# Block-sparse attention and a gated convolution FFN on one core: the same steps in a new written order

## The chip, the cores and the metric

The kernel runs on one core of a Trainium2 chip. Five engines of the core take part: TensorE (PE) multiplies matrices, VectorE (DVE) and ScalarE (ACT) compute element by element and move data between memories, GpSimd (POOL) starts loads, SyncE (SP) starts stores and transposing transfers. Each engine works through its own list of instructions in order; semaphores make one wait for another. The metric is device time in microseconds, median of three runs: 207.86 (207.11 to 208.13).

## The reference

Two operations, one after the other. The first is attention over 4 batches, 8 heads, 768 positions, head size 64, with a mask by blocks of 32 positions:

```python
scores = scale * np.matmul(q, k.transpose(0, 1, 3, 2))
mask = np.abs(blk_i - blk_j) <= 1          # neighbours, first and last block,
mask = mask | ...                          # and three sampled blocks per block row
attn = softmax(np.where(mask, scores, -1e9))
x = np.matmul(attn, v)                     # heads side by side: (4, 768, 512)
```

The second is a feed-forward network whose hidden layer is gated by a convolution over three positions:

```python
h = np.maximum(x @ w_in, 0.0)              # (4, 768, 1024)
conv_out = sum(conv_w[k] * hp[:, k:k + S, :] for k in range(3))
gate = 1.0 / (1.0 + np.exp(-conv_out))
out = h * gate @ w_out                     # (4, 768, 512)
```

## The kernel before

**Tiling.** Heads go in 16 pairs, four pairs to a batch. The output positions go in segments: each batch has two halves of 384 positions, and the last half of the last batch is cut in 256 and 128, nine segments in all. Within a segment, blocks of 128 keys by 128 queries are taken eight at a time; such a *unit* has one score tile `st` of 1024 columns. There are 144 units, 18 to a whole segment.

**A unit.** TensorE computes its scores from the slot `t` of the head pair, which holds transposed K and Q with 24 rows of mask appended (L762, two steps `s` of four blocks). ACT takes the exponential into `pt` (L774). TensorE multiplies by V (L799, two steps `av` of four matmuls with 65 columns, the 65th being the sum). When a head pair of a segment is done, DVE takes the reciprocal (L707) and normalises (L709) into `xtok`.

**Ahead of the units.** POOL's queue loads K, Q and V with a cast to bf16 (`nat`, `nq`, `vn`; L239). For the first six pairs TensorE transposes K and Q (L460, L500, L522) and DVE or ACT copies them into the slot (L331, L327). For the other ten, SP's queue transposes them by DMA into `stg` (L597), and DVE copies from there. V is copied to `vt` (L327 on ACT, L331 on DVE). Mask rows are computed on DVE at the start (L299 and others), written back once by SP to `mback` (L343), and filled into reused slots from there.

**The FFN.** `xtok` is transposed to `xT`, by TensorE for the first and the last two segments (L728, with a copy on ACT or DVE), by SP's DMA otherwise (L718). The first FFN matmul (L896) goes to a `mix` tile; ReLU copies it to `hE`, on ACT (L916) or DVE (L918). DVE makes three products with the convolution weights (L954) and two sums (L962), ACT a tanh (L1001), DVE the rest of the gate (L1004) and the gate product `gT` (L1009). For the last, 128-wide segment TensorE does the convolution itself with diagonal matrices (L379 makes them, L973 uses them). The second FFN matmul (L831) goes to `mix` again (to `st` for the last block); an output copy by ACT (L327) or DVE (L331) brings it to `o2s`, and SP stores it (L840).

**Buffers.** PSUM holds two `st`, two `av` and two `mix` tiles. `mix` is shared by transposes and both FFN matmuls.

**The order.** The code first builds a graph of 1,787 steps and then emits them by a written list: `ORDER` is a text in which two characters name a step, one may choose the engine, and one chooses the buffer. `put_down` reads it from left to right. What each engine does in which order is set by this text alone; nothing is planned at run time. At the start TensorE has 13 matmuls on zeros with 256 columns and 32 with 128 (L230); the text places these fillers too. POOL has `pace` copies between its loads (L407, L673): tiny copies that wait for an exponential or for an earlier load, so that loads start no earlier.

Of the kernel before, what the change touches and what calls it, by code (L numbers as in the profile page):

```python
# [22 lines left out]
1SA05j11V15k0E5g15c05d1Y05l211V18V191WV11XV5o05p5q35h1k15i0F1+V1ZV5t15u0G5m0H5n5C05D1O02k1/12d22x31b1a2v21l24V1  # L23
0I0J5r5v45s4S5E55H15I2702a15M05N5J05O10K5R15S5T25w5x15F5G28V22bV2cV29V5+05/5K5L5P6035y02iV21t5z1o631642l1654680
692o05Q6d16e5U2mV32nV2pV2qV6a55V5A16i06j6f06106266671c5W12y5BV06r16s6k11u1P06b6c4T2r34U2J04V2L04W1v2M6t26w05X6x
6y36g2016h6B16C6D46l1RV1QV2wV36m16G06H6u1s1n6v6z5Y06I51p4X1w4Y2X14Z1x4+2Z14/2+501y511z5234222V5ZV21V6n26P16Q6R0
6A6E6F6U06V6J6K1j6o6L06M6p06W16S06Z16+6T6N16qV6OV1r6/2720732e02fV2gV743ih16X77178iiik07f07g794il1q7k17l7h51i
ijV002KV47m0in16Y707p07q7r1imViF0iGiHiI71ioipV17u17v7w2iJiq0ir7C075762z1isViK2AV42BV7D7H17I7E32C07a7b17i7j7niN1
7c17J42s17M07N2tV7o7s7t7x537R17S2DV2uV2EViO147y7O57z2iP7AiQiz1iLiR7T03007W07X7Y17diAit082183iBA2842iu870887F17G
ivV37K7L2N18938c18d7PiM07Q7U7V2OV02PViw07e1iS312/18h0ixiyV8i7Z7+0852Q17/0iV2iW8e48j58p18q3823j38r0868a8b8f8u08v  # L30
2SViT80iYiX8w18g8k8l8z18A2RV7BiC08s18B28E08FiD8G3iU8J18K8L4iEVj918R08S8tja8x8T58y8C8D8W18H8X8I36254378/090iZi+
j13jf0jg8Y09112YV0j28m18nj4j333V32Vi/941958M8N08U8V8Z8+92939c09d962j5j01mj63919h19ijh979e498jbj7j89j5ji158O29m0
9n9r19sjc818ojjA09o1jdA13ajo0jp9w09t29909a35V18P3f3g33cV3bV553i3d0562F057jl1jmjnA9x9E19FjqV3eV2jJ08Q23k09y3ju0
jv9f09g9J0jKjM9K9G0jLjwVjN9k9l9p3h3o2T13p19q9L49O19Pjr19u2G09T09U9v9z2HV2IV9Q5jO9B19Cjs9/1jx09A19V2jyjzAa0a139D
9b3r3s0jtVjR1jSjP3w1jUjA1jBa402U0jCA3l9Ha5a91aaa619I9M9NjD1jEae09Raf9Sab42VV2WVaj1jFAjZ2jTjVjQj+ag53u3tjWak9W9X
jG0a20jH9Y2k09Zj/al0jIAar0a3a7a8kv13Dacasadaw1axjXjYkj0ahat3ay1aB0aiamaCan1auavkk3E13G3Ak1k53k6k7k8k9k29+k3k4
aD4kaaG1aHao1azaAkwaI5aO0aEaFaPklkx3B23F3M3N0aQ2aT1aUaV0kbkckmknV23nVapaJkyaY0aZb11b2aK3v43xkzA33qV33zV3yVa+3
b31kE0kFkB1kCb60b7aR0aS3H0aL0be1kDV14kGAkZ0k+k/l0kK0kLbfaWb84kMAbg5kH1kIbj0kJV53I1bkkQ0l1bl2kRkSAbo1kT13P3Q23S
kAjekobpaXbt0a/bub0b4l2bq03mVaMl51l6bv3kN0kOb5kUl8kPV6ld2bB1bCb9ba1bb2bD1kVA7kW0bG0bHbhkXbI4bibmbnbL1brl73R3XbM
bcbsbwbxbQ0bRaq03T0jkaNkYAbN5bS2kd1bd3JbE0bFkebV1bWkp0lelfl9lall3c10l3lg3CV4lhkqbJbKkrl41by1lbbObPbX0c2c61lic33  # L40
3UkfkgkhA3bzlmljlolnlplcc7c813OV0bAkslqlk3LVbTbUlz1bYcb0ccbZ1c4cg1lrls3KV3VV13WVcd4ktA1b+0b/c5c9cachci5lAlBcelC
lDA2co0cpct1cfculI0lF1lGlHVlJlKVm10cjm2m4cq0cv3cy0czm3m5cD1ckcEcA4cF53+3/343403Y141kilt1lL0cr0cl2cmcI0lMlNAcscJ
lulO0lPcwcQ1cK2cR4c4d0m6lQVm91mam7mbmcm8cS1lvlwcxcV0cWcBcCcG3ZV1c+1c/cHlxA0cX3d04lR0cL42494hd30d4c01441cN1mdcO
d50lSlU1cM1lTAlVdb1dccTcUmelWVmh2mimfdg0lX0dhl+1mklYl/dd5lZVdl1cYcZdi2d1dmd2d6d7de0m0Adn1cnmjmgku4i0dq0drd80mp3
d9mrmlmqmsmx0ds3lE4e4fdv1mtdwmD1dfdx4mmmElycP45dD0dEdI1djdkdF5dodpdtdJdudymydN0dadz1dGdHdOmnmudK24q4r1dP1dA2mo
mFmzdBmvmwdS1dT46V247VdU3mAmBV34a24gd+0d/mGdLe31dMdQe4mHV1e04e52dC24jmY0e80mV1e9mWdRed1dVeemZdW4v4n4s4tea04E4F2
mXV08m+VdX1nh0njdY4w1ei0n21n3ejm/0n0ef5e10eq1ere2e6e7ebdZmI4o0ek14Jn1A94bV2ev0n50ecewes4ninkn4Anlegehex2np1el
em1eA1eBeC0en0nq4kV3eonsepn6etn7Aaeun81n9eF0eGeN1eOnaAnx2eyezeDnb0nceH5eS0eEeTeInrnt4lVeP1eJne1eX1eYeQ0eK2eL4u
4m4xnyndAbeU4eZ2nmnunznfnAmJ0mKeRngVnF3nGnB4pV3f00eVeMmLf1f51eWf6nvnnnHno0f25mP1mQmMfd0fef71mNA2ff4nCnInwnJ4yV4
mRe+e/fi1mSfjf34zVnDmTA0fn0f4o30o4fk2o5Ao61foo7fs1ftfp54G4Bo8Vot0ounEov4C14H4I4PnKnL4Q2fu3nN0nOf8f91fa1nMnT1ow  # L50
fA0fBnUfgnPfF1nVmC4K0484LoxfbfC04DA4fGfH1oyfhnQnRV1fK0nWflfLnZ0fmnXV3n+fc04RV0oz4MV04NVo01o1fP1fM4fQfU0fqfrfvfV
fwn/Ao2AfR2oAol1omfx0onfW5oofyopfD0oc0g01g1g23o91fEodg50oeAg6g70oqfInSoafJobVoB2oDoCof0ga1fNgbfOgc1fSoggf0ggoi1
# [1005 lines left out]
```

## Time and profile before

| | |
|---|---|
| median of three runs | 207.86 us (207.11 to 208.13) |
| profiled execution, first to last instruction | 205.4 us; the page has no other time for it |
| median less span | 2.46 us |
| TensorE busy | 197.1 us |
| ACT busy | 189.7 us |
| DVE busy | 184.9 us |
| POOL busy | 59.4 us |
| moved by DMA | 25.6 MB |

In the profile a row of the timeline gives start, duration, engine, line, operation, output and input, and the count of instructions that it merges. A row of the windows gives the stretch, its length, then busy time and count for each engine, the granted TensorE clock, the DMA share and the rate. A row of the groups gives line, engine, shapes and count, then busy time and the mean of one in ns, then the idle time ahead and what ended it. The chain of waits lists pieces that follow one another, each freed by the one ahead. TensorE's matmuls overlap: each lasts longer than the distance to the next.

### The profile page before, as it was taken

What the parts mean: (1) busy time and instruction counts of PE and PEld (TensorE: products, weight loads), DVE (VectorE), ACT (ScalarE), POOL (GpSimd) and SP (SyncE); (2) the same over time, 40 slices, a digit from 0 to 9 for tenths busy, and PEclk for the clock granted to TensorE, in tenths of its full rate; (3) what the DMA queues carried; (4) which work ended last, traced back from release to release, by engine and by line L of the source; (5) the groups of instructions that cost most, each with busy time, mean ns of one, the idle gap of its engine ahead of it and who ended that gap; (6) DMA issues with size and microseconds to landing.
All of it is one profiled execution on the core that took longest, in us unless ns stands there. A gap on an engine that the chain in (4) does not pass through costs nothing.

```text
span 205.4 us, 6237 instructions
## 1 busy us (share of the span) xinstructions
PE 197.1 (96%) x2392; PEld 142.3 (69%) x2409; DVE 184.9 (90%) x572; ACT 189.7 (92%) x253; POOL 59.4 (29%) x113
## 2 busy tenths in 40 slices
PE   7799999999999999999999999999999999999992
PEld 5677877786667766776667767766567667787760
DVE  7999999999999998999899996999999959999960
ACT  6799999999999999999999998999999978998841
POOL 8689255312831133202443253900000000000000
PEclk9999999999999999999999999999999999999999
DMA  5999999994999979999779799998053131000405
GB/s 155 196 190 154 186 178 114 197 127 88 154 150 126 125 103 138 218 166 163 95 105 226 97 117 123 175 154 126 14 174 88 21 123 51 3 2 3 153 3 204
DMA packets 50969, 25.59 MB, mean 125 GB/s; under 512 B 36764, under 2 KB 47996, under 8 KB 50940
## 3 DMA queue, kind: packets, MB, share of 16 engines
q0 software_dynamic: 19728, 11.05, 46.0%
q1 hardware_dynamic: 30924, 13.86, 31.0%
q8 instruction: 19, 0.31, 0.6%
q10 hardware_dynamic: 288, 0.30, 0.5%
q14 instruction: 10, 0.08, 0.1%
HBM read 23.09 MB, written 6.29 MB: 143 GB/s over the span
## 4 chain that ended last, share of the span: by engine, by line
PE 68%; ACT 15%; DVE 12%; issue 3%; ACTq 0%; DVEq 0%
PE st L762 22%; PE mix L896 15%; PE mix L831 15%; PE av L799 12%; ACT pt L774 11%; DVE m L954 3%; DVE t L331 2%; DVE m L962 2%; ACT m L1001 1%; DVE xtok L709 1%; PE st L831 1%; ACT vt L327 1%; DVE diag L379 1%; ACT hE L916 1%; PE mix L728 1%
## 5 line engine op out<-in xcount | busy, mean ns | idle before, releaser
L774 ACT ACTIVATE pt<-st 128x1024 bf16<-128x1024 f32 (+1 forms) x145 | 142.2, 1051 | 4.2 <-PE st L762 3.7
L762 PE MATMUL st<-t 88*128 88x256 bf16 (+2 forms) x600 | 90.5, 267 | 2.3 <-DVE t L331 1.2
L799 PEld LDWEIGHTS <-pt 128*128 128x128 bf16 x1152 | 54.0, 97 | 14.2
L762 PEld LDWEIGHTS <-t 88*128 88x128 bf16 x600 | 48.9, 97 | 21.0 <-issue 1.9
L799 PE MATMUL av<-vt,pt 128*128 128x65 bf16 x1152 | 60.5, 193 | 0.1
L896 PE MATMUL mix<-xT,winb 128*128 128x384 bf16 (+2 forms) x288 | 55.2, 307 | 0.1
L954 DVE TENSOR_SCALAR m<-hE,cw 128x382 bf16<-128x382 bf16 (+2 forms) x192 | 49.1, 312 | 0.4 <-ACT hE L916 0.2
L831 PE MATMUL mix<-woutb,gT 128*128 128x512 bf16 x167 | 47.2, 379 | 0.7
L962 DVE TENSOR_TENSOR m<-m 128x764 bf16<-128x764 bf16 (+2 forms) x64 | 34.1, 532 | 0.6
L896 PEld LDWEIGHTS <-winb 128*128 128x128 bf16 x288 | 24.0, 97 | 9.2 <-issue 0.6
L1001 ACT ACTIVATE m<-m 128x764 bf16<-128x764 bf16 (+2 forms) x32 | 27.1, 853 | 0.0
L831 PEld LDWEIGHTS <-gT 128*128 128x128 bf16 x200 | 17.1, 97 | 10.0 <-DVE gT L1009 1.2
L407 POOL COPY pace<-pt 1x1 bf16<-1x1 bf16 x24 | 6.4, 268 | 54.1 <-ACT pt L774 54.0
L916 ACT ACTIVATE hE<-mix 128x384 bf16<-128x384 f32 (+2 forms) x39 | 19.8, 519 | 0.4 <-PE mix L896 0.2
L1009 DVE TENSOR_TENSOR gT<-m,hE 128x764 bf16<-128x764 bf16 (+3 forms) x36 | 18.2, 509 | 0.4
L709 DVE TENSOR_TENSOR xtok<-av,rcp 128x384 bf16<-128x384 f32 (+2 forms) x36 | 18.3, 507 | 0.4
L239 POOL DMA_DIRECT2D nat<-in_q_dram x23 | 17.3, 752 | 3.8 <-DMA nat<-in_k_dram 1.6
L918 DVE TENSOR_SCALAR hE<-mix 128x384 bf16<-128x384 f32 x25 | 13.7, 553 | 4.3 <-PE mix L896 3.7
L331 DVE COPY t<-mix 64x384 bf16<-64x384 bf16 (+1 forms) x33 | 13.2, 411 | 0.6 <-PE mix L460 0.2
L239 POOL DMA_DIRECT2D nat<-in_k_dram x15 | 12.0, 803 | 3.0 <-issue 2.4
L1004 DVE TENSOR_SCALAR m<-m 128x764 bf16<-128x764 bf16 (+3 forms) x36 | 11.9, 334 | 0.7 <-ACT m L1001 0.7
L327 ACT COPY o2s<-mix 128x512 f32<-128x512 f32 x15 | 9.2, 613 | 3.3 <-PE mix L831 3.2
(76 smaller groups left out, 118.2 us busy)
## 6 DMA issues: line engine op xcount, KB each, us to landing
out_dram<-o2s SPq DMA_DIRECT2D x23, 256.0 KB, 2.2
nat<-in_k_dram POOLq DMA_DIRECT2D x15, 192.0 KB, 4.5
vn<-in_v_dram POOLq DMA_DIRECT2D x15, 192.0 KB, 5.0
nat<-in_q_dram POOLq DMA_DIRECT2D x6, 192.0 KB, 4.5
winb<-in_moe_w_in_dram POOLq DMA_DIRECT2D x2, 512.0 KB, 8.4
woutb<-in_moe_w_out_dram POOLq DMA_DIRECT2D x4, 256.0 KB, 5.8
nat<-in_q_dram POOLq DMA_DIRECT2D x9, 96.0 KB, 5.1
nq<-in_q_dram POOLq DMA_DIRECT2D x6, 96.0 KB, 5.3
```

The source lines that it names most:

```text
L239: return op(name, {eng: occ}, lambda e: on(e).dma_start(out=dst(), in_=src), prio, deps, dma=(kind, service), **kw)
L709: nm = op("norm", {"DVE": t_dps(128 * C)}, lambda e: nc.vector.tensor_tensor(out=xtok_t[xk.index][:, 0:C].rearrange("p c h d -> p h c d"), ...
L762: nc.tensor.matmul(out=st[:, 128 * x:128 * (x + n_)], lhsT=t[0:88, 12 + 6 * hh + kc, :], rhs=t[0:88, idx:idx + (n_ - 1) * (2 if P < NPE el ...
L774: nc.scalar.activation(out=pt_t[ptb.index][:, c0:c1], in_=st_t[stb.index][:, c0:c1], func=AF.Exp, bias=0.0, scale=0.125)
L799: nc.tensor.matmul(out=o[:, off:off + 65], lhsT=pt_t[ptb.index][:, 128 * x:128 * x + 128], rhs=V_t[vslot_b[P].index][:, hh, kc, 0:65], sta ...
L831: nc.tensor.matmul(out=acc(), lhsT=gT_t[gb.index][:, ffc, 128 * t:128 * t + 128], rhs=woutb[:, ffc, c0:c1], start=(ffc == 0), stop=(ffc == ...
L896: nc.tensor.matmul(out=mix_t[hb.index][:, w1 * y:w1 * y + w1], lhsT=winb[:, fc, 128 * ffc:128 * ffc + 128], rhs=xT_t[xt_buf[n].index][:, f ...
L916: nc.scalar.activation(out=dst, in_=src, func=AF.Relu, bias=0.0, scale=0.5)
L954: nc.vector.tensor_scalar(out=m_t[cb.index][:, x, y, 0:w], in0=hE_t[heb.index][:, f0 + y, t0 + x:t0 + x + w], scalar1=cw[:, x, f0 + y:f0 + ...
L962: nc.vector.tensor_tensor(out=m[:, a_, :, 0:w], in0=m[:, a_, :, 0:w], in1=m[:, b_, :, 0:w], op=ALU.add)
L1001: th = [op("tanh", {"ACT": t_act(2 * w) + 0.04}, lambda e, cb=cb, w=w: nc.scalar.activation(out=m_t[cb.index][:, 0, :, 0:w], in_=m_t[cb.in ...
L1009: nc.vector.tensor_tensor(out=gT_t[gtb.index][:, f0:f0 + 2, t0:t1], in0=m_t[cb.index][:, 0, :, 0:w], in1=hE_t[heb.index][:, f0:f0 + 2, 1 + ...
```

## The change

The text `ORDER` is replaced. It names the same 1,787 steps, each once; no step, shape or dependence is added or removed, and the code around the text is unchanged (the text is one line shorter, so every line number below it is one lower).

What differs, read from both texts:

- The order of the steps on all five engines.
- The engine of 48 steps. At the start, two mask copies and both Q casts, one Q copy and one K copy go from DVE to ACT, one mask copy, one K cast, one K copy and the first V copy from ACT to DVE. Later, ReLU goes from ACT to DVE in 14 places and the other way in 10, the output copy in 6 and 4, the copy of transposed attention output in 2 and 1, one V copy from ACT to DVE.
- The place of the fillers on TensorE, and of loads on POOL's queue: the later Q halves of the first two pairs stand ahead of the K of the third pair.
- SP's queue: the write-back of mask rows stands behind the first transpose of attention output.
- The buffer numbers that go with these.

```diff
 ORDER = """
-000211g010M030405060708090a0S0T1T01U230251262h12j20U0L0O0N0P0Q0R0b0c0d0e0f0g0h0i0j0k0W1e0V0X12V13A17V1AV30Y1CA
-1DA1f1d1E01K10l1H01FA00Z1LV10V0/A0m0n0o0p0q5805911JV1BV1h1GA1IA0r0s0t0u0v1M05a05b0w0x0y0z0A0B0C0D5e05f1NA0+16V
...
-q/r0r1A0r2
+0M0L0S00010211f0N0T0O031T2040W0P05060Q071U1d12A0U08090R0a13A1O21e0b0V0c0d1g1AA11h23117V0e1CA0f0g0h0Y0i0j0k1/11E0
+1BA1K10Z0l1FA00m0n1M02531LA10V0/V1NA2d31DV1GA5800+5a41H0265910o0p16V11A0q0r0s0t1IV5e02h25b0u1i0v18V0w5f0x191JA0y
...
+rtr5rurx3rL0qXrGqYrSryr6rzrDrMrEr7A0rHrIr8rNrJV1qZ1rTq+rKrOq/rPA2rUrQr0rVVr1A0rWr2
 """
```

More of the change, by code (lines that the diff above doesn't have):

```diff
@@ L26 @@
[L26 to L40, printed above, removed]
@@ new lines @@
+6s2X26c5X6g6h6t16w01o6x6l6m05Y06y06n06B15ZV6C1m6u6v2e06D26G02fV6H6o6z2016I16A2gV6P16Q1t6E6F6p06R422V6J4Z6U01x6qV
+6V21V6K6W36L26Z16M6+6S16T6/56N06X6Y6OV720731qih07441c77178ik1ii7921nil4+ijV1b2Z17f07gimA1p70717h07k1iF17l4/7576
+iGin07m17a7p0iI7b07q2KV0iq17r27c17u1iH7vio7dir7w4iJ7e07C07DisV2+7i7j7E57nipV97H17I501y7o147siN32s07J07t7M02uV51
+7N1ziO7x2z13007O32tV7R1iQ7S7y2N02AV47T17W07X2BV7F17G7K2OV07Y27L821837z22PV2Q17P528407Q3412SVit02RV8707A2C1iK88
+2EV8c17Biu2DV53360895iP7U8diw1ivVhix8e3iR8h0548iiyV7V7Z7+08j4858p1iV28q31867/18a2YV38b8r28fiL8u0iW8viz1808w52/1
@@ new lines @@
+3B23v4ar0asj/acjWadahk03ljHjD19Zat5jEjXaw1jIVai3xaxjFAamk1an13Gay2auaB0k52aCavkv1jY9+aD13Fazk6aAaG1aHk7kj0k2k8
+3j3aO0aEaI4kkk9aFaPk3kw3qV1kak43MaJaT1aKaQ5aUkbklkckxaV4aL0ao1aY0apaZkm3nVa+2aq1aR03Pb113Q3b2kyb303N0aSaWkzV2jk
+b60aXa/knA0b73yVb0be1b82bf3mVkB03zVb4b5kN1bg1aM3I1bj03SbkkCbl0b9kObb1kDV0ibo13H0ba1bpkPAbbcbh3Rbibq3bt0aNkQ0kRbm
+bnkSVbu3XkE13T0bv23CV4bB1ld0kFkK03OV0kGAlfbCbr3JbG0bD1kZ2bsbwkH1k/bHbxk+kLbI2kIkMVbE0bL1bMby2kJA3bzkT0bN3kUl53bA
+bFbJbQ0l0bRkVA7kW1lebS5bV1l1bdbWkd0l7bX4bKkX3+lg3/2bOkekolhl2kf3Ul6bPc10likYVc2kg3LVc33c61c7ll1bTbUkp1lnc85cb0l8
@@ new lines @@
+kql9bYkhA1cc43bZ13Y2ljcg1cd4krb+0l33KVlF040ksb/lachl40lGci0c4co0lbc5lHVc9cpcalmcecq1ct1cflccjculI0ktV0cv3ckcy0lJ
+lkkulO13ZV2lKA41c02cr03VV1czlPcA53WVlL0cD1lokAcElMlQAm104414ccscF44d1cwlNVcxcI0cJlpcBlt1cK0m3lz0cl2cCcmcQ1lqcRm2
+cG42lAcS5m4cHcL49cV0cWm5lucX44hlrlvcN0lsc+14i04ec/m6cOlBm924a1lwd01malCm7cM1d30lxA0mbd4db1lDV3d52dclylR1cnmclS
+lU0dd3mdlVlWV45cTdg04fmecUdhlTVdl1cYdi5dmcZmh3d1d2lEl+0midn4lX1cPmjdq0drmkd6lYds0m84qd74r3l/mlde0dfm0Adv1lZVdwmm
+dD04gdEmfdjd81dkdx1dod9mx0mgdpdamD1dF5mp0dI1dtmrdJdudydK3mqdz1dN04vdOmsdGdHmy4sdP5mndS1mtdT4n4jdL4o0dA2dMmomumE
```

45 lines of the change are left out of this document (22 added, 23 removed).

## The prediction

> **What bounds the kernel now.** I read the page's busy shares and chain first, then the chain's pieces for TensorE's pace, then the windows of each matmul line, last the two ends in the timeline.
>
> ```profile
> span 205.4 us, 6237 instructions
> PE 197.1 (96%) x2392; PEld 142.3 (69%) x2409; DVE 184.9 (90%) x572; ACT 189.7 (92%) x253; POOL 59.4 (29%) x113
> ...
> PEclk9999999999999999999999999999999999999999
> ...
> PE 68%; ACT 15%; DVE 12%; issue 3%; ACTq 0%; DVEq 0%
> ```
>
> Three engines are above 90%, and the chain passes through all three, so shares alone do not name the bound. A busy TensorE need not be at its peak, so I take its pace from places where it runs unhindered:
>
> ```profile
> 29.42 0.65 PE mix L896 x4
> 40.35 0.48 PE av L799 x16
> 55.78 0.88 PE st L762 x8
> 94.63 0.86 PE mix L831 x4
> 34.31 0.34 PE mix L460 x6
> ```
>
> Pieces of the chain do not overlap, so these give the pace: a 384-column matmul 0.65/4 = 0.163 us, an AV matmul 0.030, a whole unit of scores (eight blocks, 1024 columns, four pieces here) 0.44, a 512-column output matmul 0.215, a 128-column transpose 0.057. Now the work after the first FFN matmul. The windows below are, in order, those of the score, AV, first and second FFN line; the last figure pair in brackets is the count of weight loads (matmul records are a few short on the fourth line, 183 of 200).
>
> ```profile
> 28.30:202.00 173.70, 77.35 (x513) 41.63 (x512) 1.00 0.73 116
> 28.30:202.00 173.70, 52.52 (x1000) 47.21 (x1000) 1.00 0.73 116
> 28.30:202.00 173.70, 55.18 (x288) 24.00 (x288) 1.00 0.73 116
> 28.30:202.00 173.70, 48.45 (x183) 17.09 (x200) 1.00 0.73 116
> ```
>
> 22 of 144 units are scored before that window, so 122 x 0.44 = 53.7. AV: 1000 x 0.030 = 30.0. First FFN: 224 x 0.163 + 32 x 0.11 (256 columns) + 32 x 0.057 = 41.8. Second: 184 x 0.215 + 16 x 0.11 = 41.3. The written order has 42 transposes and 24 convolution matmuls more: 66 x 0.057 = 3.8. Sum 170.6 us. What time was there for it?
>
> ```profile
> 28.38 0.48 PE L896 MATMUL mix<-xT,winb 128*128 128x384 bf16 x2
> ...
> 199.43 2.32 PE L831 MATMUL mix<-woutb,gT 128*128 128x512 bf16 x10
> 201.79 0.58 ACT L327 COPY o2s<-mix 128x512 f32<-128x512 f32 x1 [1.14 <-PE mix L831]
> ```
>
> The first FFN matmul starts at 28.38, the last matmul's result is there at 199.43 + 2.32 = 201.75; a unit alone shows 0.60 where its pace is 0.44, so 0.16 of that is drain. 201.59 - 28.38 = 173.2. TensorE is thus at 98.5% of its pace, and **the order can win at most 2.6 us there**; the rest must come from the 28 us ahead or the 3.6 us behind (205.4 - 201.8).
>
> **The change, part by part.** Every instruction is kept, so TensorE's demand is the same. Order, engine and buffer numbers change.
>
> *The head (ahead of the first FFN matmul).* Nothing but scores and AV can run there, and scores are paced by the exponentials.
>
> ```profile
> 6.21 0.40 ACT L327 COPY t<-mtok 24x256 bf16<-24x256 bf16 x1 [1.08 <-DVE mtok L299]
> ...
> 8.63 0.47 ACT L327 COPY t<-av 64x384 bf16<-64x384 bf16 x1
> 9.13 0.83 ACT L327 CAST vt<-m 128x768 bf16<-128x768 f32 x1
> 9.87 8.34 ACT L774 ACTIVATE pt<-st 128x1024 bf16<-128x1024 f32 x9
> ```
>
> From 9.87 on ACT issues exponentials without a gap (9 in 8.34, one every 0.92). In the new order the V cast (0.83) is on DVE; between the first two exponentials and the train stand a mask copy (nearest row 0.40) and a K copy (0.47, as before). The train starts 0.83 - 0.40 = 0.43 us earlier if the first exponential is not later. ACT gets more ahead of that one (a mask copy, both Q casts, another Q copy, less one K cast, one K copy and one mask copy), about 0.7 us by rows of 0.40 to 0.70, and it had 1.08 us of idle there. So it fits.
>
> DVE gives the other end:
>
> ```profile
> 0.00:28.30 28.30, 24.85 (x345) 20.07 (x346) 25.61 (x85) 24.88 (x32) 20.05 (x37) 1.00 1.13 177
> ```
>
> DVE (third pair) is busy 25.6 of 28.3 and makes the Q and K copies for each next pair just in time. The new order takes ten steps out of its list ahead of the first FFN input and puts ten others in; with the V cast between its 0.35 (row of the bf16 copies below) and 0.83, the list becomes 0 to 1 us lighter, but the cast stands before the copies of the second head pair. If those come late the train stops: I take that as a loss up to 0.4. Between +0.4 and -0.43 I take **-0.3**, nearer the second, since ACT's rows show the removed cast directly and DVE's list gets no longer.
>
> The new order also has 40 AV steps (of four matmuls) done before the first FFN matmul where the old had 38: 8 x 0.030 = **-0.24** us of work that no longer lies behind.
>
> *POOL's loads at the start.* Two loads of later Q halves are moved ahead of the K of the third pair.
>
> ```profile
> 3.94 0.73 POOL L239 DMA_DIRECT2D nat<-in_k_dram  x1
> ...
> 6.78 0.76 POOL L239 DMA_DIRECT2D nq<-in_q_dram  x1
> ...
> 14.11 0.50 PE L460 MATMUL mix<-ident,nat 128*128 128x128 bf16 x6
> ...
> 14.61 0.18 POOL L673 COPY pace<-nq 1x1 bf16<-1x1 bf16 x1 [0.65 <-DMA nq<-in_q_dram]
> ```
>
> That K is issued two places later, 3.94 + 1.45 = 5.4. The Q half issued at 6.78 had landed by 14.6, so 7.8 us is the longest a load takes there: landed by 13.2, read at 14.11. Cost nothing, cover 0.9 us; beyond it, each late us stops TensorE for one.
>
> *SP's queue.* The write-back of mask rows moves behind the first activation transpose, and three row fills behind later transposes.
>
> ```profile
> 40.88 1.18 SPq L718 DMA_TRANSPOSE xT<-xtok  x1
> 42.16 1.24 SPq L597 DMA_TRANSPOSE stg<-nat  x1
> 43.58 2.57 SPq L239 DMA_DIRECT2D t<-mback  x3
> ...
> 51.24 1.12 DVE L331 COPY t<-stg 64x1536 bf16<-64x1536 bf16 x2
> ```
>
> The first fill's slot gets its K and Q from DVE's staging copies at 51.24, and scores read it after that (in both orders at the 90th of 288 score steps). The write-back (two issues) and a transpose ahead push a fill from 43.6 to about 46. Cost nothing, cover 5 us.
>
> *Work moved between ACT and DVE.* After the head 14 ReLU copies go from ACT to DVE and 10 back; output copies 6 and 4, attention-output copies 2 and 1, one V copy to DVE.
>
> ```profile
> L916 ACT ACTIVATE hE<-mix 128x384 bf16<-128x384 f32 x31 | 15.8, 524 | 0.1
> L327 ACT COPY o2s<-mix 128x512 f32<-128x512 f32 x15 | 9.2, 613 | 3.3 <-PE mix L831 3.2
> L327 ACT COPY vt<-vn 128x768 bf16<-128x768 bf16 x1 | 0.9, 919 | 0.0
> ...
> L918 DVE TENSOR_SCALAR hE<-mix 128x384 bf16<-128x384 f32 x25 | 13.7, 553 | 4.3 <-PE mix L896 3.7 <-ACT pt L774 0.5
> L331 DVE COPY o2s<-mix 128x512 f32<-128x512 f32 x8 | 5.5, 690 | 2.9 <-PE mix L831 2.9
> L331 DVE COPY vt<-vn 128x768 bf16<-128x768 bf16 x14 | 5.0, 354 | 0.0
> ```
>
> ACT: -4 x 0.52 - 2 x 0.61 - 0.92 = -4.2 us; DVE: +4 x 0.55 + 2 x 0.69 + 0.35 = +3.9 us (the single attention-output copy is left out, under 0.4). On the path lies only what TensorE waits for:
>
> ```profile
> PE st L762 <- ACT pt L774: 0.6, 2, 0.4
> ```
>
> That bounds the gain from a lighter ACT at 0.6; I take **-0.3**, half, because the relief is partial: among the exponentials 24 to 75 ACT keeps 7 of 11 ReLUs and 2 of 3 output copies. DVE's +3.9 I cost at nothing: it is busy 184.9 of 205.4, and its idle time from 28.3 to the last gate product at 198.1 (row below), 169.8 - (184.9 - 25.6) = 10.5 us, covers it (below for the case that it does not).
>
> *Distance from scores to AV.* Counting TensorE's own work, at the paces above, between the end of a unit's scores and its first AV matmul: for the units after the head the old order leaves 1.57 us at least, 4.3 in the median, and under 1.9 for one unit; the new order 1.35, 3.0, and under 1.9 for fourteen.
>
> ```profile
> L774 ACT ACTIVATE pt<-st 128x1024 bf16<-128x1024 f32 x143 | 141.1, 1057 | 4.2 <-PE st L762 3.7 <-ACT hE L916 0.3
> ```
>
> Drain and exponential need 0.16 + 1.06 = 1.22. With ACT free every unit still fits; each 0.25 us that ACT is behind costs the fourteen 0.4 us in all, 0.45 costs 1.3, 0.6 costs 2.6. Bounds 0 and 2.6; I take **+0.4**, since half of one ReLU (0.52) ahead of the exponential is what an engine at 92% shows on average.
>
> *The tail.* The last gate product ended at 197.65 + 0.43, with 3.5 us of TensorE work behind it; in the new order only 1.3 us (two output steps of 512, two of 256 columns). Cost nothing, cover 2.2 us less.
>
> ```profile
> 197.65 0.43 DVE L1009 TENSOR_TENSOR gT<-m,hE 128x512 bf16<-128x512 bf16 x1
> ```
>
> **The sum.** -0.3 - 0.24 - 0.3 + 0.4 = -0.44, so a span of 205.0. The median of the runs is 207.86, 2.46 over the span; with that, 207.4 us.
>
> **Rivals.** (1) *The order closes the remaining gaps*: half of the 2.6 us goes, the head gives its 0.43 + 0.24, the AV distance costs 0.2: 207.86 - 1.3 - 0.67 + 0.2 = 206.1; all of it gone 204.8. For it: DVE idles 4.3 us ahead of its ReLUs for TensorE, so evacuation has room. Against it: nothing that can be read off the order shows those gaps closed.
>
> (2) *Slower: AV waits for exponentials.* Place: the fourteen units above, between units 37 and 137. With a ReLU and more (0.6) ahead of each exponential 2.6 instead of 0.4: 209.6; with 0.7, 211. It decides from 0.53 on, where 1.9 outweighs the gains by the margin that counts. For it: ACT has 92%, its row names waits of only 4.2 us in all. Against it: fewer ReLUs on ACT.
>
> (3) *Slower: DVE becomes the bound.* If the +3.9 is not absorbed, the last gate ends up to 3.9 late against 2.2 of cover and every gate ahead of it delays output steps: 1.7 at the end alone, 3.9 at most; 209.1 to 211.3. It decides from a DVE idle of under 2 us.
>
> (4) *TensorE's clock.* Its start shows a second pace:
>
> ```profile
> 1.06 3.29 PE L230 MATMUL av<-warm 128*128 128x256 bf16 x19 [1.06 <-DVE warm L223]
> ...
> 7.01 0.60 PE L762 MATMUL st<-t 88*128 88x384 bf16 x4 [1.25 <-DVE t L331]
> ```
>
> 13 matmuls of 256 columns and 6 of 128 took 3.3 us where the pace above gives 13 x 0.11 + 6 x 0.057 = 1.8, although the granted clock reads 1.00; the gap of 1.25 us behind them did not bring it back. The new order spreads its filler matmuls differently and waits for a K cast that ACT does later. A longer gap that brought the slow pace back for as long would cost 3.3 - 1.8 = 1.5: 208.9. The Trainium skill (TensorE: Matmul & The Clock Gate, The HAM clock gate) states such a halved clock until about 3.4 us of activity, and again after an idle window of that length; the trace agrees as far as it goes, since 1.25 us did nothing. I see no gap over some 1.5 us in the new head.
>
> **How the numbers follow.** Forecast 0.40, rival (1) 0.29, (2) 0.20, (3) 0.08, (4) 0.03. Half a per cent, 1.04 us, is about what a measurement tells from none. The forecast lies within it (207.4, its own range 206.8 to 208.9): same 0.40, faster 0.29, slower 0.31. The range runs from 205.8, part of the way into (1), to 210.0, past (2)'s 209.6 and part of (3); outside lie about a quarter of (1) and a third of (2) and (3).
>
> **What would show it.** First FFN matmul near 28.1 instead of 28.38; ACT busy near 185 and DVE near 189; TensorE's waits for ACT's exponentials appear on the AV line (rival 2) or not; waits for DVE's gate products on the output line (rival 3); a TensorE idle of over 3 us in the head, or matmuls there at half pace (rival 4). The prediction is wrong if the work after the first FFN matmul takes less than 172 or more than 175 us.

## The result and the profile after

The changed kernel takes 210.12 us in the median of four runs (209.29 to 211.0), the kernel before 207.63 beside it: a ratio of 1.012, 95% interval 1.0075 to 1.0165. It is slower by 1.2%, where the forecast was 207.4, no slower than before, and its range ended at 210.0. A second measurement of the same kernel (`after_again` below) gave 210.18 and 1.0135 (1.0113 to 1.0158). The profiled execution took 210.92 with a span of 209.1. Line numbers are one lower than before.

The page's first lines, clock and chain after the change:

```profile
span 209.1 us, 6173 instructions
PE 200.1 (96%) x2392; PEld 143.3 (69%) x2409; DVE 188.0 (90%) x578; ACT 189.5 (91%) x247; POOL 63.0 (30%) x113
...
PEclk9999999999999999999999999999999999999999
...
PE 35%; DVE 33%; ACT 20%; DMA 5%; issue 4%; POOL 1%; SPq 0%; ACTq 0%; POOLq 0%; DVEq 0%
```

The busy shares are those of before. The chain is not: TensorE's share fell from 68% to 35%, and DVE's rose from 12% to 33%. That points to DVE as what TensorE now waits for; the experiments below test it. The DMA share is not there in the chain of a second profile of this kernel (DVE 42%, PE 36%).

The two ends, from the timeline of the changed kernel (first FFN matmul; last output matmul; last output copy):

```profile
30.03 0.49 PE L895 MATMUL mix<-xT,winb 128*128 128x384 bf16 x2
...
204.88 0.59 PE L830 MATMUL mix<-woutb,gT 128*128 128x512 bf16 x2
205.56 0.58 ACT L326 COPY o2s<-mix 128x512 f32<-128x512 f32 x1 [0.75 <-PE mix L830]
```

The first FFN matmul starts at 30.03 instead of 28.38: 1.65 us are lost ahead of it. From there to the end of the span it takes 179.07 us instead of 177.02, 2.05 more. The windows from the first FFN matmul to the end (length, then busy time of PE, weight loads, DVE, ACT, POOL), of the changed kernel and of the kernel before:

```profile
30.03:209.10 179.07, 172.66 (x2040) 121.60 (x2054) 163.33 (x494) 163.15 (x214) 43.27 (x75) 1.00 0.73 113
```

```profile
28.38:205.40 177.02, 172.12 (x2049) 122.18 (x2063) 159.22 (x488) 164.78 (x222) 39.31 (x76) 1.00 0.72 116
```

DVE got 4.1 us heavier (forecast 3.9), ACT 1.6 lighter (forecast 4.2). DVE still has 15.7 us of idle there, 9.8 of them ahead of the end of the last gate product at 202.07 (before: 10.9). The chain of this profile names two late loads as well (start, length, what):

```profile
1.66 4.36 DMA o2s<-in_q_dram
...
60.69 5.33 DMA nq<-in_q_dram
```

### The profile page after: what moved, and what is told of

It is laid out like the page before. It is cut to its first block, busy times and chain, and to the rows that moved or that the text cites. A ratio compares the mean times of both kernels' runs of the same rounds, so it can differ in the third digit from the quotient of the medians.

```text
span 209.1 us, 6173 instructions
## 1 busy us (share of the span) xinstructions
PE 200.1 (96%) x2392; PEld 143.3 (69%) x2409; DVE 188.0 (90%) x578; ACT 189.5 (91%) x247; POOL 63.0 (30%) x113
## 4 chain that ended last, share of the span: by engine, by line
PE 35%; DVE 33%; ACT 20%; DMA 5%; issue 4%; POOL 1%; SPq 0%; ACTq 0%; POOLq 0%; DVEq 0%
ACT pt L773 16%; PE mix L830 10%; PE st L761 10%; DVE m L953 9%; PE mix L895 8%; DVE t L330 6%; DVE m L961 5%; PE av L798 5%; DVE hE L917 3%; DMA nq<-in_q_dram 3%; DVE xtok L708 2%; DVE gT L1008 2%; DMA o2s<-in_q_dram 2%; DVE m L1003 2%; ACT m L1000 2%
## 5 line engine op out<-in xcount | busy, mean ns | idle before, releaser
L761 PE MATMUL st<-t 88*128 88x256 bf16 (+2 forms) x600 | 94.1, 269 | 1.0 <-ACT pt L773 0.3
L798 PEld LDWEIGHTS <-pt 128*128 128x128 bf16 x1152 | 56.5, 97 | 17.0 <-ACT pt L773 0.8
L798 PE MATMUL av<-vt,pt 128*128 128x65 bf16 x1152 | 63.9, 193 | 0.5
L761 PEld LDWEIGHTS <-t 88*128 88x128 bf16 x600 | 47.7, 98 | 18.1 <-issue 1.4
L895 PE MATMUL mix<-xT,winb 128*128 128x384 bf16 (+2 forms) x288 | 56.3, 307 | 1.3 <-DVE t L330 0.8
L830 PEld LDWEIGHTS <-gT 128*128 128x128 bf16 x200 | 17.1, 97 | 10.9 <-DVE gT L1008 1.4
L406 POOL COPY pace<-pt 1x1 bf16<-1x1 bf16 x24 | 8.3, 344 | 53.8 <-ACT pt L773 53.8
L915 ACT ACTIVATE hE<-mix 128x384 bf16<-128x384 f32 (+2 forms) x35 | 17.5, 505 | 0.8 <-PE mix L895 0.7
L917 DVE TENSOR_SCALAR hE<-mix 128x384 bf16<-128x384 f32 x29 | 15.7, 550 | 1.8 <-PE mix L895 0.9
L238 POOL DMA_DIRECT2D vn<-in_v_dram x15 | 12.2, 815 | 2.4 <-DMA nat<-in_k_dram 1.8
L330 DVE COPY t<-stg 64x1536 bf16<-64x1536 bf16 x20 | 11.4, 573 | 0.3
```

The costliest lines, as they stand in the source:

```text
L238: return op(name, {eng: occ}, lambda e: on(e).dma_start(out=dst(), in_=src), prio, deps, dma=(kind, service), **kw)
L330: nc.vector.tensor_copy(out=dst, in_=src)
L761: nc.tensor.matmul(out=st[:, 128 * x:128 * (x + n_)], lhsT=t[0:88, 12 + 6 * hh + kc, :], rhs=t[0:88, idx:idx + (n_ - 1) * (2 if P < NPE el ...
L798: nc.tensor.matmul(out=o[:, off:off + 65], lhsT=pt_t[ptb.index][:, 128 * x:128 * x + 128], rhs=V_t[vslot_b[P].index][:, hh, kc, 0:65], sta ...
L830: nc.tensor.matmul(out=acc(), lhsT=gT_t[gb.index][:, ffc, 128 * t:128 * t + 128], rhs=woutb[:, ffc, c0:c1], start=(ffc == 0), stop=(ffc == ...
L895: nc.tensor.matmul(out=mix_t[hb.index][:, w1 * y:w1 * y + w1], lhsT=winb[:, fc, 128 * ffc:128 * ffc + 128], rhs=xT_t[xt_buf[n].index][:, f ...
```

## Experiments

Times are medians; the ratio stands against the kernel before, run on the same chip beside each. "The rest" is the stretch from the first FFN matmul to the end of the span, of the profiled execution.

### Which part: old head with new rest, and the other way round

```diff
-ORDER = the new text
+ORDER = the old text up to the first FFN matmul, then every other step
+        in the order and on the engine of the new text (16 buffer numbers renumbered)
```

> The old order up to the first FFN matmul, then all other steps in the new order and on the new engines. Theory A (the loss of 2.5 us lies in two places: about 1.65 ahead of the first FFN matmul, less 0.24 for the AV done early, and about 2.1 behind it): first FFN matmul near 28.4, work behind it some 2 us longer than the old 173.2, total 207.6 + 2.1 = 209.7. Rival (the late head upsets what follows, and the rest in itself is as good as the old): 207.6.

Measured: 209.63, ratio 1.011 (1.0082 to 1.0138). The new rest behind the old head loses 2.2 us, but not all of it is the new rest's own. Its first FFN matmul comes at 29.33, not near 28.4, because at the seam it waits for DVE's slot copies, which it does in neither kernel:

```profile
29.33 0.49 PE L896 MATMUL mix<-xT,winb 128*128 128x384 bf16 x2 [0.71 <-DVE t L331]
```

The stretch behind it takes 178.1, 1.1 more than before.

```diff
-ORDER = the new text
+ORDER = the new text up to the first FFN matmul, then every other step
+        in the order and on the engine of the old text (13 buffer numbers renumbered)
```

> The new order up to the first FFN matmul, then all other steps in the old order and on the old engines. Theory A: first FFN matmul near 30.0 when TensorE's clock comes late, total 207.6 + 1.65 - 0.24 = 209.0, and run times in two groups some 1.7 us apart, as the changed kernel's are. Rival (the late head is made good by what follows, since the exponentials have caught up): 207.6 to 207.9.

Measured: 211.65, ratio 1.019 (1.0158 to 1.0223), 2.6 above the expectation. The new head with the old rest is worse than the whole change. In its profile, of its slowest run (212.21), the granted clock is full only from 13.2 us on, the first FFN matmul comes at 31.12, and the rest takes 178.7, 1.7 more than in the kernel before. The two halves don't add up to the whole, so they do not measure the two losses one by one.

The changed kernel once more, for a second profile:

> The changed kernel itself, unchanged, beside which the edits of it are read: 209.3 to 211.0. If its two groups of times come from the head (Q load landed late and clock late, or both early), a profile of the faster group shows the first FFN matmul near 28.9 and about 179 us from there to the end of the span, and one of the slower group near 30.0 with the same 179.

Measured: 210.18, ratio 1.0135 (1.0113 to 1.0158); this profile is of a run of 209.49. First FFN matmul and the window behind it:

```profile
28.79 0.49 PE L895 MATMUL mix<-xT,winb 128*128 128x384 bf16 x2
```

```profile
28.79:207.70 178.91, 172.63 (x2040) 121.66 (x2054) 163.16 (x494) 163.12 (x214) 43.48 (x75) 1.00 0.71 114
```

The rest is the same within 0.2 us (178.91 and 179.07) while the head moved by 1.24. So the difference between these two runs lies in the head, and the loss has two parts: 1.9 to 2.05 us in the rest in both profiles, and 0.4 to 1.65 us in the head.

### The rest: engines alone

```diff
 ORDER = the new text
-39 steps behind the head on their new engines (ReLU, output copies, ...)
+the same steps, in the same places, on their old engines
```

> The new order throughout; behind the first FFN matmul each step is on the engine that the old order gave it (39 steps: ReLU, output copies, copies of transposed attention output, one V copy). Theory T1 (DVE, given 3.9 us more work, is late with the copies that free the mix tiles): the loss of 2.1 us behind the first FFN matmul goes for the most part, 208.0 to 208.6. Rival T2 (the places of transposes and FFN matmuls make TensorE wait for DVE whichever engine copies): 209.5 to 210.5, or more since ACT then is late.

Measured: 214.55, ratio 1.0339 (1.031 to 1.0368).

```diff
 ORDER = the old text
-39 steps behind the head on their old engines
+the same steps, in the same places, on their new engines
```

> The old order throughout; behind the first FFN matmul each step is on the engine that the new order gives it. T1 (the engines alone make DVE late): 209 to 209.7. T2 (the places do it): 207.4 to 207.9.

Measured: 222.37, ratio 1.0736 (1.0699 to 1.0773). Neither theory gave such numbers. Summing in both traces TensorE's delays of 70 ns and more behind 31.5 us (the distance to the next matmul beyond the pace of its columns, put down to what the next one waits for; where a matmul's record is missing from the trace, its 0.215 us are taken off), the old order with new engines has 11.2 us by DVE and 6.0 by ACT, the new order with old engines 3.2 and 5.1. In these two mixtures the order and the engines of its copies can't be told apart; they don't show what either is worth.

### The rest: less work on DVE

```diff
-nc.vector.tensor_scalar(out=m_t[cb.index][:, x, y, 0:w], in0=hE_t[...][:, f0 + y, t0 + x:t0 + x + w], ...)
+v = w // 4 if x == 2 else w
+nc.vector.tensor_scalar(out=m_t[cb.index][:, x, y, 0:v], in0=hE_t[...][:, f0 + y, t0 + x:t0 + x + v], ...)
...
-nc.vector.tensor_tensor(out=m[:, a_, :, 0:w], in0=m[:, a_, :, 0:w], in1=m[:, b_, :, 0:w], op=ALU.add)
+v = w // 4 if b_ == 2 else w
+nc.vector.tensor_tensor(out=m[:, a_, :, 0:v], in0=m[:, a_, :, 0:v], in1=m[:, b_, :, 0:v], op=ALU.add)
```

> The changed kernel with less work on DVE behind the first FFN matmul: the third tap of the convolution is multiplied and added on the first quarter of the columns alone (its product and sum are left out on the rest), some 19 us less of DVE by its rows, everything else the same. Theory T1 (behind the head TensorE loses 2.1 us because DVE reaches the copies that free mix tiles, and gate products, late): the stalls of 0.2 to 0.7 us at 37 to 137 us go, the work behind the first FFN matmul takes 173 us instead of 175.5, median 207.6 to 208.2. Rival T2 (the places of steps on TensorE, whose inputs would be late with any DVE): 209.5 to 210.1.

> The kernel before with the same part of the third tap left out. TensorE had only 2.6 us to win behind the first FFN matmul, and its stalls by DVE there are some 1 us: 206.4 to 207.2. With T1 the distance between this kernel and the changed one with the same cut is that of the heads alone, 1.4 us or less; with T2 it stays 2.5.

Measured: 207.84 with the new order, ratio 1.0028 (0.9999 to 1.0056), and 207.33 with the old one, 1.0001 (0.999 to 1.0012). The edit took 11.4 and 11.7 us of work off DVE, less than the 19 expected. The twelve runs with the new order lie between 206.89 and 210.11, three of them above 209; those with the old order between 207.19 and 207.88. The rests, new order and then old:

```profile
28.94:205.60 176.66, 172.18 (x2057) 121.80 (x2054) 151.56 (x494) 162.44 (x214) 40.20 (x76) 1.00 0.75 116
```

```profile
28.19:205.30 177.11, 172.92 (x2066) 122.19 (x2063) 147.61 (x488) 164.69 (x222) 38.48 (x76) 1.00 0.69 116
```

A lighter DVE gives the new order 2.25 us of its rest (178.91 to 176.66) and the old order nothing (177.02 to 177.11). The two medians, 2.9 us apart without the edit (210.18 and 207.31), are 0.5 apart with it. That is the clearest result of this study: in the new order DVE's lateness accounts for the rest's loss; in the old order less DVE work gains nothing. The chain of the new order with less DVE work reads like that of the kernel before:

```profile
PE 67%; ACT 14%; DVE 9%; DMA 5%; issue 2%; SPq 1%; ACTq 0%; DVEq 0%
```

The delays, summed as above:

```
                          by DVE      by ACT
before                    0.3 us      1.6 us
after                     3.3         0.6
after, less DVE work      1.0         0.8
before, less DVE work     0.5         1.5
```

The stretches of 10 us show how DVE's idle time is spread. Before (busy PE, weight loads, DVE, ACT, POOL; the third is DVE):

```profile
68.00:78.00 10.00, 9.75 (x127) 6.65 (x128) 8.79 (x26) 9.98 (x14) 3.62 (x8) 1.00 0.94 127
```

After:

```profile
68.00:78.00 10.00, 9.91 (x140) 7.33 (x139) 9.93 (x30) 9.88 (x12) 2.85 (x6) 1.00 1.14 156
78.00:88.00 10.00, 9.83 (x120) 6.79 (x119) 7.77 (x20) 9.33 (x13) 3.27 (x7) 1.00 0.95 149
...
98.00:108.00 10.00, 9.83 (x119) 6.81 (x119) 9.90 (x27) 9.45 (x13) 4.72 (x8) 1.00 0.80 145
...
138.00:148.00 10.00, 9.95 (x111) 6.49 (x111) 9.94 (x29) 10.00 (x14) 0.00 (x0) 1.00 0.81 127
...
168.00:178.00 10.00, 10.00 (x107) 6.94 (x106) 7.25 (x24) 7.96 (x11) 0.00 (x0) 1.00 0.42 143
```

Of the 17 stretches from 28 to 198 us DVE is busy for 9.8 us or more in ten after the change, in three before. The line at 9.8 favours this reading: at 9.7 it is ten and seven. Its idle time is gathered in a few others (2.2 and 2.75 us in the two shown). Stretches this long do not say where the waits are: only about half of the 3.3 us of delays lies in the ten full ones. Shorter ones do: in the 5 us ahead of each of the thirteen delays by DVE, DVE is busy for 96 to 99%. A full DVE alone is not enough for a delay, since the kernel before has full stretches too and hardly any delay; in the new order TensorE needs a copy at such a place. One of them in the changed kernel, DVE and then TensorE:

```profile
40.68 0.55 DVE L330 COPY t<-mix 64x768 bf16<-64x768 bf16 x1
41.15 0.18 DVE L706 RECIPROCAL rcp<-av 128x6 f32<-128x6 f32 x1
41.36 1.20 DVE L330 COPY t<-mix 64x768 bf16<-64x768 bf16 x3
```

```profile
40.89 0.33 PE L521 MATMUL mix<-ident,nat 128*128 128x128 bf16 x3
41.06 0.41 PE L798 MATMUL av<-vt,pt 128*128 128x65 bf16 x8
41.97 0.49 PE L895 MATMUL mix<-xT,winb 128*128 128x384 bf16 x2 [0.51 <-DVE t L330]
```

The transposes of one pair's K and Q fill both `mix` tiles; DVE is behind with the copies, and the FFN matmul waits 0.51 us for a tile.

### The rest: can the lateness be moved away?

Three attempts, each on one side of the wait. First TensorE's side, with the new and with the old head:

```diff
 TensorE, the new rest, at ten of its stalls (example: 41.97 us):
-..., q_tr, av, av, f1 (waits), s, ...
+..., q_tr, av, av, s, f1, ...
```

> The changed kernel with thirteen steps of TensorE shifted by one to three places at ten of its stalls behind the head (a waiting FFN matmul or transpose behind the score and AV steps that follow it, one output step ahead of a waiting score); every other engine's order is the same. If DVE's lateness hits TensorE only where a step stands too early: about half of the 3.1 us of these stalls goes, median 208.6 to 209.2. If DVE (in order, nearly full) is what sets the time, the wait comes back at the next step that needs it: 209.8 to 210.3.

> The old head, then the new order, with the same thirteen steps shifted. Places: 208.1 to 208.7 (209.6 less 1 to 1.5). DVE: 209.4 to 209.8.

Measured: 211.61, ratio 1.0189 (1.0146 to 1.0232), and 210.92, 1.017 (1.0141 to 1.0199); 1.4 and 1.3 slower than without the shifts. In the profiles, of the fastest run of each (210.26 and 210.68), the delays by DVE are 2.8 us in both, those by ACT went up to 1.7 and 1.3.

Then DVE's side:

```diff
 DVE, the new rest, seven copies (example: 103 us):
-..., g2, g1, relu, mul, g2, output copy (late), ...
+..., g2, output copy, g1, relu, mul, g2, ...
```

> The changed kernel with DVE's list alone changed: seven late steps that TensorE waits for (three ReLU, two output copies, two copies of transposed Q) stand one to three places earlier, ahead of products and sums whose readers come later; one V copy stands later. If the order of DVE's list is what makes TensorE wait: 1.0 to 1.7 of the 2.1 us behind the head go, median 208.5 to 209.2. If it is the amount of work on DVE at these places (98% busy and more), the wait comes back at the gate products: 209.7 to 210.3.

Measured: 211.56, ratio 1.0196 (1.0158 to 1.0234), 1.4 slower. The delays by DVE are 3.7 us. The copies are earlier, and other readers wait, as this row of the waits shows (us in total, times, longest), which the changed kernel doesn't have:

```profile
PE av L799 <- DVE xtok L709: 0.6, 1, 0.6
```

Last the amount at four places:

```diff
 output copies and ReLU at 103, 113, 136 and 156 us:
-DVE
+ACT, behind the exponential that runs at that time
```

> The changed kernel with four of the late copies (two output copies, two ReLU, all between 102 and 157 us) on ACT instead of DVE. Less work on DVE there: the four stalls (0.23, 0.19, 0.30, 0.14 us) go, 209.3 to 209.7. If ACT then is late with exponentials by as much: 210 or more.

Measured: 209.9, ratio 1.0108 (1.0077 to 1.0139). The delays by DVE fell from 3.3 to 2.3, those by ACT rose from 0.6 to 1.1, the rest is 0.4 to 0.6 shorter (178.5). Over the runs, 0.2 to 0.3 us against the changed kernel is less than their spread, so this points to the amount and doesn't show it. Together: these moves of the wait along either list made the kernel slower, and less work on DVE removes most of the wait. Which single steps would have to leave DVE, without ACT being late for them, stays open.

### The head: clock, Q load, or the order

In the profile with the span of 209.1 us ACT waits for a load ahead of its second Q cast, and TensorE's fillers go at 0.107 us each (0.64 us to the next row for six), though the granted clock reads 1.00. ACT, then TensorE, of the changed kernel:

```profile
6.05 0.35 ACT L326 CAST nat<-o2s 128x192 bf16<-128x192 f32 x1 [1.00 <-DMA o2s<-in_q_dram]
...
10.38 1.02 ACT L773 ACTIVATE pt<-st 128x1024 bf16<-128x1024 f32 x1
11.70 2.85 ACT L773 ACTIVATE pt<-st 128x1024 bf16<-128x1024 f32 x3 [0.29 <-PE st L761]
```

```profile
8.32 0.85 PE L229 MATMUL av<-warm 128*128 128x128 bf16 x6
8.96 0.63 PE L761 MATMUL st<-t 88*128 88x128 bf16 x2
```

In the kernel before eight fillers at that time take 0.46 us, 0.057 each:

```profile
8.11 0.62 PE L230 MATMUL av<-warm 128*128 128x128 bf16 x8
8.57 0.86 PE L762 MATMUL st<-t 88*128 88x128 bf16 x6
```

In the second profile of the changed kernel the load came earlier and the pace is full (the six fillers' 0.50 us hold 0.16 of drain, which leaves 0.057 each):

```profile
5.35 0.35 ACT L326 CAST nat<-o2s 128x192 bf16<-128x192 f32 x1 [0.30 <-DMA o2s<-in_q_dram]
...
9.65 3.77 ACT L773 ACTIVATE pt<-st 128x1024 bf16<-128x1024 f32 x4
```

```profile
7.29 0.50 PE L229 MATMUL av<-warm 128*128 128x128 bf16 x6
8.03 0.38 PE L761 MATMUL st<-t 88*128 88x128 bf16 x2 [0.24 <-ACT pt L773]
```

The starts of the third and the 23rd exponential, read from the single instructions, split the head:

```
                       third    23rd    between   first FFN matmul
before                  9.87    28.66    18.79     28.38
after, run of 210.92   10.38    30.29    19.91     30.03
after, run of 209.49    9.65    29.05    19.40     28.79
```

Even in the better case the exponentials take 0.61 us more: six of them come 0.06 to 0.36 us later than the pace of 0.92, 1.14 in all, where the old order has two such places (0.05 and 0.47). Five more traces of the old head take 18.5 us between these two exponentials, so the difference is 0.6 to 0.9. In the other case the start is 0.73 later, and the fourth exponential waits 0.4 more.

The clock, by wider fillers:

```diff
-def warm_mm(e, n=256 if x < NWARM else 128):
+def warm_mm(e, n=256 if x < NWARM + 9 else 128):
```

> The changed kernel with nine of its start fillers (the six behind the first 13 matmuls on zeros, and the three ahead of the third transpose) 256 columns wide in place of 128, so that TensorE has no gap of 0.2 us or more between 1.06 and 7.2 us. Theory T3 (TensorE's clock is raised late, at 10.4 us, because two gaps of 0.46 and 0.22 us fall into the stretch that decides it): matmuls at full pace from 7.2 at the latest, first FFN matmul near 28.7 instead of 30.03, median 208.7 to 209.3, and no runs near 211. Rival T4 (the late head is ACT's list, whatever the clock): first FFN matmul near 30, median near 210, run times still in two groups.

Measured: 210.31, ratio 1.0138 (1.011 to 1.0165), run times from 209.3 to 211.0. In the profile the pace is full by 5.5 us, as intended, yet the first FFN matmul comes at 29.84, because the Q load was late:

```profile
6.41 0.35 ACT L326 CAST nat<-o2s 128x192 bf16<-128x192 f32 x1 [1.35 <-DMA o2s<-in_q_dram]
```

The late load alone thus costs about 1 us: the third exponential is at 10.69, and the 23rd follows 19.41 later, as in the better case. The clock alone is not the cause. Side by side, the profiles of the new head (start of the second Q cast; time from which the granted clock stays full; third exponential; from there to the 23rd):

```
                                   Q cast        full clock    third          to the 23rd
early load, four profiles          4.96 to 5.35   4.4 to 5.5    9.60 to 9.75   19.40 to 19.48
late load, five profiles           5.98 to 6.46  10.4 to 13.2  10.25 to 10.73  19.79 to 20.77
late load, wide fillers            6.41           5.3          10.69           19.41
```

The four are the second profile of the changed kernel and those of less DVE work, of the shifted steps on TensorE and of the earlier Q load; the five are the first profile and those of the old rest, of the late copies first, of the four copies on ACT and of the old engines. A load that lands late moves the start by as much. In all five profiles with the fillers as they are the full clock then comes late too, or falls back, and that costs another 0.4 to 1.4 us; with wide fillers, in one profile, it did not.

ACT's list:

```diff
 ACT: ..., first Q cast, first K cast,
-second Q cast (waits), copy of K, copy of Q, copy of Q's second half
+copy of K, copy of Q, second Q cast, copy of Q's second half
```

> The changed kernel with ACT's second Q cast behind the first K copy and the first Q copy, and the second Q copy behind it, so that ACT isn't held 1.0 us by that Q load. T4: the first exponential at 7.6 or earlier instead of 8.04, first FFN matmul some 0.4 us earlier, median 209.6. T3 (the clock): first exponential moves by 0.1 at most, median 210.1 with two groups of times as before.

Measured: 210.46, ratio 1.016 (1.0126 to 1.0194). The first exponential is at 8.03, no earlier than the 8.04 of the slower profile: the cast still stands ahead of it, now at 6.24, and TensorE's transpose of that half ahead of the first score. The move was too small to tell T4 (ACT's list) from T3 (the clock). Here the load had landed early, at 5.34. The run showed something else, TensorE's pace falling back (windows of TensorE; the value behind the count is the granted clock):

```profile
6.50:8.00 1.50, 1.12 (x11) 1.00 1.23 180
8.00:9.50 1.50, 1.50 (x13) 0.50 1.37 203
9.50:11.00 1.50, 1.50 (x15) 0.50 1.42 194
11.00:12.50 1.50, 1.50 (x19) 0.87 1.41 184
```

The load's place:

```diff
 SP: load of K's first half,
-sampled blocks, second Q half
+second Q half, sampled blocks
```

> The changed kernel with SP's load of the second Q half issued ahead of the load of the sampled blocks (0.46 us earlier). If the late start (third exponential at 10.38) comes from ACT waiting for that Q load: the wait of 1.0 us ahead of the second Q cast falls to 0.5 or less, third exponential at 9.7 to 9.9, TensorE has no gap there and its clock is full by 6 us more often, first FFN matmul near 29.0 to 29.4, median 209.0 to 209.5. Rival (landing time is set by the traffic, not by the issue; or the masks, now later, hold the scores): 210 to 210.5.

Measured: 210.6, ratio 1.0135 (1.0097 to 1.0173), run times from 209.5 to 212.9. The profile is of the 209.52 run and agrees with the theory (no wait for the Q load, third exponential at 9.75, first FFN matmul at 28.93), but that is the fastest of its runs, and the median did not move. Where the load landed in the others was not traced, so whether an issue 0.46 us earlier makes it land earlier stays open. The direct test, the second Q cast back on DVE in the new order, was not run.

The old start ahead of the new head:

```diff
-ORDER = the new text
+ORDER = the old text up to the fifth score step, then all other steps of the new text
```

> The old order up to the fifth score step (first three exponentials), then the new order and engines. The changed kernel's head was late by 1.63 us at its 23rd exponential: 0.51 at the third (ACT held for a Q load), 0.39 behind it (clock), 0.73 in fixed waits of the later exponentials. Theory (these three are independent): third exponential at 9.9, first FFN matmul near 29.1, median 209.2, without a group near 211. Rival (the later waits come from the late start): first FFN matmul near 28.4, median 208.3.

Measured: 212.03, ratio 1.023 (1.0197 to 1.0264), which neither theory gave. In its profile TensorE waits 0.77 us for a slot copy on DVE ahead of 14.0 us, the granted clock is 0.50 from 7.3 to 10.7, and the first FFN matmul is at 30.95. This mixture has troubles of its own and tells nothing of the three parts.

The price of a late clock, in the old order:

```diff
-def warm_mm(e, n=256 if x < NWARM else 128):
+def warm_mm(e, n=16 if x < NWARM + 6 else 128):
```

> The kernel before with its first 19 matmuls on zeros only 16 columns wide, so that TensorE is nearly idle until 4.3 us and its clock can't be raised by then. If a late clock is worth what the changed head shows (a wait of ACT for scores of 0.3 to 1.3 us ahead of the fourth exponential where the trace has half pace until 10.4 to 13.2 us): first FFN matmul at 28.7 to 29.7 instead of 28.4, median 207.7 to 208.7. Rival (the head is paced by exponentials whatever the clock): 207.3.

Measured: 208.73, ratio 1.0058 (1.004 to 1.0076): a late clock costs 1.3 us. The third exponential is at 10.88, the first FFN matmul here:

```profile
29.52 0.48 PE L896 MATMUL mix<-xT,winb 128*128 128x384 bf16 x2
```

And the gap in the old head, filled:

```diff
-def warm_mm(e, n=256 if x < NWARM else 128):
+def warm_mm(e, n=256 if x < NWARM or 19 <= x < 25 else 128):
```

> The kernel before with the six fillers that stand between its third transpose and the first score 256 columns wide instead of 128, which fills 0.3 us or more of TensorE's gap of 1.25 us there. If some of its runs (near 208.4) are those in which the clock is late or falls back: no run above 207.8, median 207.1 to 207.4. Rival: as before, 207.1 to 208.5.

Measured: 207.33, ratio 0.9984 (0.9965 to 1.0004), all twelve runs between 207.14 and 207.82, where the kernel before beside it reached 209.18. The median is the same. That the old kernel's own high runs are those with a late clock is in agreement with this, and no trace of such a run was taken.

No version beat the kernel before. With its DVE lightened by 11.7 us the kernel before ran no faster, so the amount of work on DVE does not bound it.

## Why the prediction was wrong

**The head, -0.3: failed.** Measured +1.65 and +0.41 in the two profiles. The list was read for its durations: a cast less, so the exponentials start 0.43 earlier. In the better run they did start 0.22 earlier. Three things were missed. First, the second Q cast had moved from DVE, where the kernel before does it after its load has landed, into ACT's list ahead of the first exponential:

```profile
7.29 0.33 DVE L331 CAST nat<-o2s 128x192 bf16<-128x192 f32 x1
```

That ACT "had 1.08 us of idle there" counted the work and not what it waits for. With the load at 6.03 the start is 0.73 later than with the load at 5.32. Second, the late clock, rival (4). Its price of 1.5 is near the 1.3 of the starved old kernel; in the slower profile of the changed kernel the exponentials behind the start took 0.5 more, which is put down to it. Its condition was wrong: no gap over 1.5 us was needed. The slower profile has gaps of 0.46 and 0.22 us among half-pace matmuls; the better one has 0.45 and 0.15, and there the clock came in time, so such gaps make a late clock possible and not certain. Third, that ACT issues exponentials without a gap was taken over from the old order; the new one holds them back six times, for 0.61 us more than the old.

**AV steps done early, -0.24: not contradicted.** With a light DVE the new rest is 0.45 shorter than the old, which can contain it; no run shows the term by itself.

**POOL's loads at the start and SP's queue, nothing: right.** No wait for the third pair's K or for a mask fill shows. But one Q load further on is in the chain now (60.69, 5.33 us), and TensorE waits 0.3 us for it; the later order of POOL's queue was not looked at.

**ACT lighter, -0.3, and distance to AV, +0.4.** Delays by ACT behind the head fell from 1.6 to 0.6 us, a larger gain than taken; whether the fewer ReLU copies or the order did it is not shown. Weight loads of AV steps wait for an exponential at three places (0.8 us in all, none before), but no AV matmul is delayed there by 70 ns or more. Rival (2) did not happen. ACT's busy time over the whole span stayed at 189.5 us instead of falling to near 185.

**DVE +3.9, costed at nothing: the step that failed.** DVE's lateness cost some 2 us behind the head, shown by the two lightened kernels. The 10.5 us of idle that were to cover it were a total over 170 us; a full engine that works in order has no use for idle time that lies 30 us further on. Whether the 3.9 us themselves or the places at which the new order needs DVE made it late is not separated; the four copies moved to ACT point to the amount. Rival (3) named the mechanism ("every gate ahead of it delays output steps") and gave 209.1 to 211.3. That this holds the result is partly luck, since 0.4 to 1.65 us of the loss come from the head. Its condition was wrong: it was to decide from an idle time of under 2 us, and DVE has 9.8 up to its last gate product. Its place was wrong too: the end lost nothing; the waits lie between 37 and 157 us, and they are for tiles that a copy must free more than for gates.

**The tail, nothing: right, though its cover was misread.** The 1.3 us were counted on TensorE's list from the place of the last gate product; on the chip DVE was ahead of that place. The product ended at 202.07, 3.2 us ahead of the end of TensorE's work less its drain (before: 3.5):

```profile
201.78 0.29 DVE L1008 TENSOR_TENSOR gT<-m,hE 128x260 bf16<-128x260 bf16 x1
```

From the last output copy's end to the end of the span there are 2.96 us, before 3.03.

**From span to median, 2.46: too large.** It set the median of 207.86 against the profile of a faster execution. In the later runs, executions of the kernel before with a span of 205.4 took 207.3 to 207.4 us, 1.9 to 2.0 more. With that the forecast would have been 0.5 lower, and further from the result.

In sum 2.3 us for the better head: 0.41 + 1.89; 3.7 for the other: 1.65 + 2.05, where -0.44 was forecast. The prediction's own sign of being wrong came true: its measure of the work behind the first FFN matmul, which was 173.2 before and was to stay between 172 and 175, is 175.3 and 175.1 in the two profiles. The two rivals that were given the least chances, (3) and (4), happened together in the slower profile, the clock at a third of its price.

## What to carry to other kernels

Read the idle time of an engine that works in order in the few microseconds ahead of each step that others wait for, not as a total, before extra work on it is called hidden. To test it, take work off the suspected engine in both versions: if one gets faster and the other doesn't, that engine's work is the difference. When a step moves to another engine's list, look at what it waits for as well as how long it takes, and don't judge an order apart from its engine choices.

## What was unexpected of the hardware

TensorE's pace can be halved again without one long gap. With the second Q cast later, it had gaps of 0.46, 0.63 and 0.24 us between 4.6 and 7.6 us, and then the granted clock was 0.50 from 8.0 to 11.4 us (rows above); the kernel before kept the full pace over gaps of 0.20 and 1.25 us. The drop lasted 3.41 us by the trace's records, and three more profiles (the old start with the new head, four late copies on ACT, the new order with old engines) show the same. An estimate from the traces: at the full pace the matmuls' columns fill 31 to 37% of the 3.41 us ahead of the drop in these four, 39% of the first 3.41 us at the full clock in the kernel before, and 46% or more in the others, which kept it. That points to the share of work in such a stretch; it is no measured threshold.

The Trainium skill (TensorE: Matmul & The Clock Gate, The HAM clock gate) has the halved clock come back after an idle window of about 3.4 us; no gap here was near that, so on this the measurement differs. The Trainium skill (TensorE: Matmul & The Clock Gate, A second HAM failure mode: psum-queue depth-cycling) tells of another kernel whose frequent short idle times between groups of matmuls made the clock go up and down; with that these runs agree. The Trainium skill (TensorE: Matmul & The Clock Gate, The HAM clock gate) also says that the window runs freely and so the moment of the full clock varies with the start; in the profiles of the new head it came (last) between 4.4 and 13.2 us.

The granted clock reads 1.00 at the start while the pace is half (six fillers in 0.64 us); the pace itself has to be looked at there.
